# Where the key norms of the first four quads stand among vector, GpSimd and activation work

## The chip, the cores and the metric

The kernel runs on one core of one Trainium2 chip. The metric is the device time in microseconds (us), as the median of a few runs. The engines are named as in the profile: PE (TensorE, matmuls), PEld (its weight loads), DVE (VectorE), ACT (ScalarE), POOL (GpSimd) and SP (SyncE, which here only issues transfers). Each engine works through its own queue in order, and waits on semaphores for the others.

## The reference

Attention with normalised queries and keys (8 batches, 12 heads, 448 positions, head size 64) feeds a feed-forward block (3584 tokens, 768 to 1024 to 768) with a softmax-weighted activation and a layer norm.

```
def rmsnorm(x, g):
    rms = np.sqrt(np.mean(x * x, axis=-1, keepdims=True) + 1e-06)
    return x / rms * g
q_n, k_n = (rmsnorm(q, g_q), rmsnorm(k, g_k))
scores = scale * np.matmul(q_n, k_n.transpose(0, 1, 3, 2))
attn = softmax(scores);  out = np.matmul(attn, v)        # then per token:
h = x @ w_in;  e = np.exp(h - h_max);  solu = h * e / sum(e)
ln = (solu - mu) / np.sqrt(var + 1e-06) * g_ln;  return ln @ w_out
```

(The softmax is written out in the original, and the last two lines are shortened.)

## The kernel before

The attention part works on **quads**: 24 of them, each of two **pairs** of heads. Quad m has the pairs a = 2m and b = 2m + 1, so pair 3 is the second pair of quad 1, and quad 0 has the pairs 0 and 1. The loop over m writes its order out by hand: the order of the calls is the order of each engine's queue. What a pair goes through, with the lines of the profile:

- `load` (L634): eight transfers of 56 KB, issued by SP, bring the queries and keys into one of five buffers. `load_v` (L647, L651) brings the values of a quad.
- `squares` (L656): ACT squares all 128x896 numbers. `row_sums` (L664): DVE sums them by groups of 32. `fold_sums` (L674, L675): POOL adds the two halves of each row for both pairs of a quad; `fold_one` (L684, L685) does that for a single pair on DVE.
- `rsqrt_seed` (L694, L695): ACT takes a logarithm and an exponential. `rsqrt_step` (L701 to L704): four small DVE instructions refine the result. These two are the norms.
- `normalise` (L713): POOL multiplies the queries and keys by the norms. `qk_transpose` (L723): DVE transposes the product. `gain` (L727): ACT scales the queries.
- `scores` (L812) and `scores_last` (L825): PE makes a score tile; ACT takes its exponential (L802). A quad has seven of these: three for pair a, one shared by both pairs (the "last", or shared one), three for pair b.
- `add` (L839): DVE adds two exponentials of a pair. `outputs` and `values` (L854, L865): PE multiplies by the values. `sums` (L884): PE sums the exponentials with a matrix of ones. `inverse` (L895, L896, and four POOL copies L903) and `divide` (L910, L911) turn the sums into factors and apply them on DVE. `store_x` (L916) writes the quad's result to memory.

Score tiles and the tile of `sums` take turns in three PSUM buffers. So the third score tile of a quad (`scores(a, 2)`) is written to the buffer that held the sums of the quad before, and waits until DVE has read that at L895. Each score tile likewise waits for the exponential three tiles back.

`unit(...)` runs one piece of PE work and then whatever `later(...)` has set for that time; the `divide` of quad m comes in that way, after the first score tile of quad m + 1. `steps_at` lists the quads in which a piece of the input weights is converted (L535, L536 on ACT, L541, L542 on DVE); from quad 2 on it is one piece in each of quads 2 to 6. From quad 5 the squares of both pairs stand together (`scarce` is then false). `early` says that a quad makes the norms of the next at its very top.

After the attention come the feed-forward products (L982, and then L1177), with PE busy throughout.

Of the kernel before, what the change touches and what calls it, by code (L numbers as in the profile page):

```python
# [366 lines left out]
def fast_path(  # L367
# [252 lines left out]
    norms = {}  # L620
# [32 lines left out]
    def squares(n):  # L653
        d = st[n]
        d["sq"] = work.tile([P, 2 * NB, 32], FP32, tag="sq", name="sq", bufs=2)
        nc.scalar.activation(d["sq"], d["qk"].rearrange("p s b d -> p (s b) d"), AF.Square)  # L656
# [3 lines left out]
    def row_sums(n):  # L660
        m, i = divmod(n, 2)
        if i == 0:
            norms[m] = {"part": small.tile([P, 2, 2 * NB], FP32, tag="part", name="part", bufs=2)}
        nc.vector.tensor_reduce(norms[m]["part"][:, i], st[n]["sq"], AX, OP.add)  # L664
# [25 lines left out]
    def rsqrt_seed(d):  # L690
        ss = d["ss"]
        p, w = ss.shape
        y = d["y"] = small.tile([P, 4 * NB], FP32, tag="ny", name="ny", bufs=2)[0:p, 0:w]
        nc.scalar.activation(y, ss, AF.Ln, scale=1.0 / D, bias=eps[0:p])  # L694
        nc.scalar.activation(y, y, AF.Exp, scale=-0.5)  # L695
# [24 lines left out]
    def qk_transpose(n):  # L720
        d = st[n]
        d["qkT"] = work.tile([P, 2, S], FP32, tag="qkT", name="qkT", bufs=3)
        nc.vector.transpose(d["qkT"].rearrange("p s t -> p (s t)"), d["qkn"].rearrange("p b d -> p (b d)"))  # L723
# [80 lines left out]
    def scores(n, kc):  # L804
        d = st[n]
        s = ps_t.tile([P, 2, 512], FP32, tag="t", name="s")

        for c in range(0, P, D):
            for h in range(2):
                hh = slice(h * D, (h + 1) * D)  # L810
                keys = slice(NJ * c + kc, NJ * (c + D - 1) + kc + 1, NJ)
                nc.tensor.matmul(  # L812
                    s[c : c + D, h, 0:S], d["qkT"][hh, 1, keys], d["qkT"][hh, 0, :],
                    start=True, stop=True,
                )
        exponentials(d, kc, s)

    def scores_last(m):

        s = ps_t.tile([P, 2, 512], FP32, tag="t", name="s")  # L820
        for i in range(2):
            for h in range(2):
                hh = slice(h * D, (h + 1) * D)
                qkT = st[2 * m + i]["qkT"]
                nc.tensor.matmul(  # L825
                    s[i * D : (i + 1) * D, h, 0:S], qkT[hh, 1, NJ * P : S], qkT[hh, 0, :], start=True, stop=True
                )
        exponentials(quads[m], NJ, s)
# [7 lines left out]
    def add(n):  # L836
        d = st[n]
        d["es"] = work.tile([P, 2, S], FP32, tag="es", name="es")
        nc.vector.tensor_tensor(d["es"], d["E", 0], d["E", 1], OP.add)  # L839
# [433 lines left out]
    def unit(f, steps=4):  # L1273
        nonlocal now
        f()
        now += steps
        due = [x for x in todo if x[0] <= now]
        todo[:] = [x for x in todo if x[0] > now]
        for _, g in sorted(due, key=lambda x: x[0]):
            g()  # L1280
# [40 lines left out]
    with tc.manual_schedule():  # L1321
# [19 lines left out]
        for m in range(NQ):  # L1341
            a, b = 2 * m, 2 * m + 1

            def outputs():
                values_last(m)
                values(a)


            next1 = m + 1 < NQ
            next2 = m + 2 < NQ  # L1350
            next3 = m + 3 < NQ
            if m == 0:
                unit(lambda: scores(a, 0))
                normalise_rows(1, 0)
                normalise_rows(1, 1)
                unit(lambda: scores(a, 1))
                unit(lambda: scores(a, 2))
                for s in range(2):
                    transpose_rows(1, s)
                    take_rows(1, s)  # L1360
                squares(2)
                row_sums(2)
                fold_one(2)
                unit(lambda: scores_last(m))
                rsqrt_seed(norms["one", 2])
                rsqrt_step(norms["one", 2])
                normalise(2)
                add(a)
                unit(lambda: scores(b, 0))
                unit(lambda: scores(b, 1))  # L1370
                unit(lambda: scores(b, 2))
                squares(3)
                add(b)
                row_sums(3)
                qk_transpose(2)
                fold_one(3)
                gain(2)
                rsqrt_seed(norms["one", 3])
                rsqrt_step(norms["one", 3])
                normalise(3)  # L1380
                load_v(1)
                load(6)
                load(7)
                for _ in range(2):
                    load_next()
                unit(outputs)
                squares(4)
                row_sums(4)
                qk_transpose(3)
                gain(3)  # L1390
                unit(lambda: values(b))
                unit(lambda: sums(m))
                inverse(m)
                later(1, lambda m=m: divide(m))
                continue
            early = 2 < m and next1
            if early:
                rsqrt_seed(norms[m + 1])
                rsqrt_step(norms[m + 1])
                normalise(a + 2)  # L1400
                normalise(b + 2)
            for x in joins_at.get(m, ()):
                combine_in(x)
            if next1:
                load_v(m + 1)
            unit(lambda: scores(a, 0))
            store_x(m - 1)
            if early:
                qk_transpose(a + 2)
                if next3:  # L1410
                    load(a + 6)
            unit(lambda: scores(a, 1))
            if m == 1:
                squares(5)
                row_sums(5)
                fold_sums(2)
            unit(lambda: scores(a, 2))
            if m == 2:
                rsqrt_seed(norms[m + 1])
                rsqrt_step(norms[m + 1])  # L1420
                normalise(a + 2)
                normalise(b + 2)
            if m == 1:
                norm_gain()
            unit(lambda: scores_last(m))
            if m < 2:
                add(a)
            unit(lambda: scores(b, 0))
            if m == 1:
                rsqrt_seed(norms[m + 1])  # L1430
                rsqrt_step(norms[m + 1])
                normalise(a + 2)
                normalise(b + 2)
                load(a + 6)
                load(b + 6)
            if m == 2:
                qk_transpose(a + 2)
                load(a + 6)
            unit(lambda: scores(b, 1))
            if early or m == 2:  # L1440
                qk_transpose(b + 2)
                if next3:
                    load(b + 6)
            if m > 1:
                add(a)
            unit(lambda: scores(b, 2))
            if m == 1:
                qk_transpose(a + 2)
            scarce = m < 5
            if next2:  # L1450
                squares(a + 4)
                if not scarce:
                    squares(b + 4)
                row_sums(a + 4)
            if next1:
                gain(a + 2)
            if m == 1:
                add(b)
                qk_transpose(b + 2)
            if next1:  # L1460
                gain(b + 2)
            if scarce:
                squares(b + 4)
                if m > 1:
                    add(b)
            if next2 and m > 1:
                row_sums(b + 4)
                fold_sums(m + 2)
            if not scarce:
                add(b)  # L1470
            add_more(a)
            add_more(b)
            unit(outputs)
            step(m - 2)
            begin(m)
            step(m - 1)
            if m - 1 in sets:
                load_next()
            unit(lambda: values(b))
            if m == NQ - 1:  # L1480
                block_sums(0, 0)
                block_sums(0, 1)
                load_x(1)
            unit(lambda: sums(m))
            inverse(m)
            if m == 1:
                row_sums(b + 4)
                fold_sums(m + 2)
            if next1:
                later(1, lambda m=m: divide(m))  # L1490
            if m == NQ - 2:
                load_x(0)
                sizes(0)
# [191 lines left out]
```

## Time and profile before

| what | before |
|---|---|
| median of 3 runs | 822.98 us (822.57 to 824.52) |
| profiled execution, its own time | 821.82 us |
| its span in the profile | 819.3 us (2.52 us of the time lie around it) |
| PE busy | 800.6 us, 98% of the span |
| DVE busy | 672.4 us, 82% |
| POOL busy | 463.6 us, 57% |
| ACT busy | 461.0 us, 56% |
| mean share of the 16 DMA engines' time | q1 52.0%, q10 4.3% |
| TensorE clock granted | 0.995 |

A profile is of one execution. The median of the runs is 1.16 us above the time of the profiled one, so sums made in the profile are compared with its own time. Times inside it are in us from the start of the span. A timeline line has the start, the length, the engine, the line, the operation, what it writes and reads, and in square brackets the idle time before it and what ended that. A wait for several semaphores is put down to the one that came last by the profile.

The PE work of a quad is the same from quad to quad, and it begins with the first score tile. By the timeline of PE these begin at 10.19 (quad 0), 25.03, 43.74, 58.44, 72.72 and 85.62 us (quad 5); after that a quad takes 12.90 us each time, to the end of the attention.

### The profile page before, as it was taken

The numbers are of one execution on the slowest core, as the hardware profiler recorded it, in microseconds if no ns is written. First come the engines' busy times: TensorE is split into PE (matmuls) and PEld (weight loads), VectorE is DVE, ScalarE is ACT, GpSimd is POOL, SyncE is SP. The second block draws the span as 40 slices with busy tenths as digits, with TensorE's granted clock in tenths as the row PEclk, the third lists the DMA queues.
The fourth block names the chain that finished last, engine by engine and source line by source line (L and its number), as shares of the span: only waits on it lengthen the run. The fifth ranks groups of instructions, "written<-read, shape, count | busy, mean of one in ns | idle before, by whom it ended". The sixth has DMA issues, their size and how long they took to land.

```text
span 819.3 us, 14945 instructions
## 1 busy us (share of the span) xinstructions
PE 800.6 (98%) x5030; PEld 470.2 (57%) x5030; DVE 672.4 (82%) x1203; ACT 461.0 (56%) x757; POOL 463.6 (57%) x635
## 2 busy tenths in 40 slices
PE   8899999999999999999999999999899999999996
PEld 4333444444344443444444444444689999999996
DVE  6679897887878878589999999999996866866945
ACT  6568777786877766355655445442425454464420
POOL 1334556455554557222254378776487867777861
PEclk9999999999999999999999999999999999999999
DMA  6778777877778654225555434542448457366312
GB/s 132 144 166 184 155 195 157 184 156 153 174 154 184 143 136 123 82 82 168 153 149 145 132 90 125 152 135 72 140 149 276 136 195 252 116 234 211 118 59 82
DMA packets 271938, 122.74 MB, mean 150 GB/s; under 512 B 190444, under 2 KB 257004, under 8 KB 271852
## 3 DMA queue, kind: packets, MB, share of 16 engines
q1 hardware_dynamic: 256668, 111.79, 52.0%
q10 hardware_dynamic: 15184, 9.90, 4.3%
q8 instruction: 42, 0.69, 0.4%
q14 instruction: 44, 0.36, 0.1%
HBM read 84.94 MB, written 36.70 MB: 148 GB/s over the span
## 4 chain that ended last, share of the span: by engine, by line
PE 88%; DVE 3%; SPq 3%; POOL 2%; DMA 2%; issue 1%; ACT 0%; DVEq 0%; POOLq 0%
PE b L982 31%; PE A L1177 14%; PE o L865 12%; PE s L812 12%; PE B L1177 7%; PE sm L884 5%; PE C L1177 3%; SPq L634 3%; PE s L825 2%; PE o L854 2%; DMA v<-in_v_dram 1%; DMA qk<-in_k_dram 0%; POOL sums L1156 0%; POOL qkn L713 0%; POOL sums L1155 0%
## 5 line engine op out<-in xcount | busy, mean ns | idle before, releaser
L982 PE MATMUL b<-w_in,xg 128*128 128x512 f32 x336 | 151.1, 592 | 0.0
L802 ACT ACTIVATE E<-s 128x896 f32<-128x896 f32 x168 | 139.1, 935 | 14.2 <-PE s L812 13.7
L812 PE MATMUL s<-qkT 64*64 64x448 f32 x1152 | 121.2, 547 | 4.0 <-DVE r L895 2.8
L982 PE MATMUL b<-w_in,xsum 128*128 128x512 f32 x252 | 115.0, 592 | 0.0
L865 PE MATMUL o<-E,v 128*64 128x448 f32 x576 | 113.5, 543 | 0.0
L982 PEld LDWEIGHTS b<-w_in,xg 128*128 128x128 f32 x336 | 63.8, 190 | 80.2 <-issue 77.1
L674 POOL COPY ss<-part 32x56 f32<-32x56 f32 x88 | 42.6, 484 | 92.8 <-DVE part L664 90.0
L713 POOL TENSOR_TENSOR qkn<-qk,ny 128x896 f32<-128x896 f32 x46 | 78.0, 1715 | 23.0 <-DMA qk<-in_k_dram 17.3
L1177 PE MATMUL A<-w_out,sums 128*128 128x192 f32 x392 | 80.8, 329 | 4.0 <-ACT u L1189 2.6
L812 PEld LDWEIGHTS s<-qkT 64*64 64x64 f32 x1152 | 48.2, 163 | 63.4 <-ACT E L802 29.0
L982 PEld LDWEIGHTS b<-w_in,xsum 128*128 128x128 f32 x252 | 47.9, 190 | 60.3 <-issue 57.4
L1060 POOL TENSOR_TENSOR he<-he,mhalf 128x1 f32<-128x1 f32 x28 | 17.1, 610 | 114.5 <-DVE he L1059 112.5
L865 PEld LDWEIGHTS o<-E,v 128*64 128x64 f32 x576 | 39.2, 137 | 72.7 <-issue 65.7
L1177 PE MATMUL B<-w_out,sums 128*128 128x192 f32 x392 | 80.1, 327 | 0.0
L1066 ACT ACTIVATE u<-u,shift,he 128x1024 f32<-128x1024 f32 x28 | 34.7, 1239 | 74.9 <-POOL shift L1062 72.3
L1177 PEld LDWEIGHTS A<-w_out,sums 128*128 128x128 f32 x392 | 66.6, 191 | 5.3 <-issue 2.9
L1177 PEld LDWEIGHTS B<-w_out,sums 128*128 128x128 f32 x392 | 66.6, 191 | 0.2
L839 DVE TENSOR_TENSOR es<-E 128x896 f32<-128x896 f32 x48 | 53.9, 1125 | 0.5 <-ACT E L802 0.5
L664 DVE TENSOR_REDUCE part<-sq 128x28 f32<-128x896 f32 x46 | 48.5, 1080 | 5.5 <-ACT sq L656 3.5
L723 DVE STREAM_TRANSPOSE qkT<-qkn 128x896 f32<-128x896 f32 x46 | 48.6, 1089 | 4.5 <-POOL qkn L713 4.5
L563 POOL TENSOR_TENSOR w_out<-w_out 128x384 f32<-128x384 f32 x44 | 50.7, 1158 | 1.9
L1177 PE MATMUL A<-w_out,s 128*128 128x192 f32 x224 | 45.8, 327 | 0.6 <-ACT u L1189 0.6
(143 smaller groups left out, 1497.5 us busy)
## 6 DMA issues: line engine op xcount, KB each, us to landing
ur<-ud SPq DMA_DIRECT2D x60, 256.0 KB, 4.4
ud<-ub SPq DMA_DIRECT2D x112, 128.0 KB, 2.3
xd<-xo SPq DMA_DIRECT2D x24, 448.0 KB, 3.4
qk<-in_q_dram SPq DMA_DIRECT2D x184, 56.0 KB, 2.3
qk<-in_k_dram SPq DMA_DIRECT2D x184, 56.0 KB, 2.2
v<-in_v_dram SPq DMA_DIRECT2D x24, 384.0 KB, 4.4
out_dram<-P SPq DMA_DIRECT2D x21, 384.0 KB, 3.5
raw<-in_moe_w_in_dram SPq DMA_DIRECT2D x12, 512.0 KB, 4.6
```

The costliest lines, as they stand in the source:

```text
L563: nc.gpsimd.tensor_tensor(o, p, q, OP.subtract)
L664: nc.vector.tensor_reduce(norms[m]["part"][:, i], st[n]["sq"], AX, OP.add)
L674: e.tensor_copy(ss[g * 32 : g * 32 + 32], part[o * 32 : o * 32 + 32])
L713: e.tensor_tensor(d["qkn"], d["qk"].rearrange("p s b d -> p (s b) d"), y.rearrange("p b -> p b ()").to_broadcast([P, 2 * NB, 32]), OP.mult,)
L723: nc.vector.transpose(d["qkT"].rearrange("p s t -> p (s t)"), d["qkn"].rearrange("p b d -> p (b d)"))
L802: nc.scalar.activation(d["E", kc], s[:, :, 0:S], AF.Exp)
L812: nc.tensor.matmul(s[c : c + D, h, 0:S], d["qkT"][hh, 1, keys], d["qkT"][hh, 0, :], start=True, stop=True,)
L839: nc.vector.tensor_tensor(d["es"], d["E", 0], d["E", 1], OP.add)
L865: nc.tensor.matmul(d["o"][h * D : (h + 1) * D, :], quads[n // 2]["v"][:, n % 2 * 2 + h, kc], d["E", kc][:, h], start=False, stop=(kc == NJ ...
L884: nc.tensor.matmul(sm[g : g + 32, :], ones[:, w], e[:, h, t * S // 2 : (t + 1) * S // 2], start=(x == 0), stop=(x == len(terms) - 1),)
L982: nc.tensor.matmul(o, a[:, c], w_in[i][:, c], start=(c == 0), stop=(c == HD - 1))
L1177: nc.tensor.matmul(k[bank], a[:, c].rearrange("p a i -> p (a i)"), w_out[:, area, i, c], start=begin and c == 0, stop=c == KC - 1, skip_gr ...
```

## The change

It moves calls in quads 0 to 3. No instruction is added, removed or reshaped, and the order on PE and on SP's queue stays as it was; the order on DVE, ACT and POOL changes.

- Quad 0: `add(a)` goes ahead of the row sums of pair 2; the squares of pair 3 go behind the shared exponential, and its row sums and norms behind the next exponentials; the transposes of pair 2 and `add(b)` come after all norms. The squares of pair 5 move here from quad 1, behind the squares of pair 4, and the row sums of pairs 4 and 5 and their fold come after `inverse(m)`; the inverse then stands directly behind the transposes of pair 3 on DVE.
- Quad 1: what moved to quad 0 is gone.
- Quad 2: the norms (and the products of pairs 6 and 7) move from behind `scores(a, 2)` to behind `scores(a, 1)`.
- Quad 3: the norms move from the top of the quad to behind `scores(a, 0)`, which puts them behind `divide(2)` on DVE; the transposes of pair 8 and `load(a + 6)` move behind `scores(a, 2)`.

```
@@ quad 0
                 squares(2)
+                add(a)
                 row_sums(2)
                 fold_one(2)
                 unit(lambda: scores_last(m))
+                squares(3)
                 rsqrt_seed(norms["one", 2])
                 rsqrt_step(norms["one", 2])
                 normalise(2)
-                add(a)
                 unit(lambda: scores(b, 0))
+                row_sums(3)
+                fold_one(3)
                 unit(lambda: scores(b, 1))
                 unit(lambda: scores(b, 2))
-                squares(3)
-                add(b)
-                row_sums(3)
-                qk_transpose(2)
-                fold_one(3)
-                gain(2)
                 rsqrt_seed(norms["one", 3])
                 rsqrt_step(norms["one", 3])
                 normalise(3)
+                qk_transpose(2)
+                gain(2)
+                add(b)
                 load_v(1)
...
                 unit(outputs)
                 squares(4)
-                row_sums(4)
                 qk_transpose(3)
                 gain(3)
                 unit(lambda: values(b))
+                squares(5)
                 unit(lambda: sums(m))
                 inverse(m)
+                row_sums(4)
+                row_sums(5)
+                fold_sums(2)
                 later(1, lambda m=m: divide(m))
                 continue
@@ quads 1 to 3
-            early = 2 < m and next1
-            if early:
+            early = 3 < m and next1
+            def norms_next():
                 rsqrt_seed(norms[m + 1])
                 rsqrt_step(norms[m + 1])
                 normalise(a + 2)
                 normalise(b + 2)
+
+            if early:
+                norms_next()
...
+            if m == 3:
+                norms_next()
             unit(lambda: scores(a, 1))
-            if m == 1:
-                squares(5)
-                row_sums(5)
-                fold_sums(2)
+            if m == 2:
+                norms_next()
             unit(lambda: scores(a, 2))
-            if m == 2:
-                rsqrt_seed(norms[m + 1])
-                rsqrt_step(norms[m + 1])
-                normalise(a + 2)
-                normalise(b + 2)
+            if m == 3:
+                qk_transpose(a + 2)
+                load(a + 6)
...
-            if early or m == 2:
+            if early or 1 < m < 4:
                 qk_transpose(b + 2)
```

More of the change, by code (lines that the diff above doesn't have):

```diff
@@ L1429, in fast_path @@
             if m == 1:
[L1430 to L1433, printed above, removed]
+                norms_next()
                 load(a + 6)
```

## The prediction

> **What bounds the kernel now.** I first read the page's busy shares and its chain of waits.
>
> ```profile
> PE 800.6 (98%) x5030; PEld 470.2 (57%) x5030; DVE 672.4 (82%) x1203; ACT 461.0 (56%) x757; POOL 463.6 (57%) x635
> PE 88%; DVE 3%; SPq 3%; POOL 2%; DMA 2%; issue 1%; ACT 0%; DVEq 0%; POOLq 0%
> ```
>
> PE bounds the whole, so only time that PE lacks in the first quads can be gained. Next, the waits of PE from 12 to 70 us (waiting engine and line, releaser, us in total, times, longest):
>
> ```profile
> PE s L812 <- DVE r L895: 2.8, 1, 2.8
> PE s L825 <- ACT E L802: 1.5, 3, 1.0
> PE s L812 <- ACT E L802: 0.6, 1, 0.6
> PE sm L884 <- DVE es L839: 0.4, 1, 0.4
> ```
>
> From 63 to 560 us PE has no wait. Quads 1, 2 and 3 take 18.71, 14.70 and 14.28 us by their first score tiles (25.03, 43.74, 58.44, 72.72), an undisturbed one 12.90: together 9.0 us over. That is the ceiling. The timelines of PE and DVE show the largest piece:
>
> ```profile
> 29.59 1.59 PE L812 MATMUL s<-qkT 64*64 64x448 f32 x8 [2.79 <-DVE r L895]
> 26.71 1.09 DVE L664 TENSOR_REDUCE part<-sq 128x28 f32<-128x896 f32 x1 [0.39 <-ACT sq L656]
> 28.13 1.11 DVE L723 STREAM_TRANSPOSE qkT<-qkn 128x896 f32<-128x896 f32 x1 [0.33 <-POOL qkn L713]
> 29.17 0.37 DVE L895 STREAM_TRANSPOSE r<-sm 128x224 f32<-128x224 f32 x1
> ```
>
> The third score tile of quad 1 waits for L895, which stands on DVE behind the transpose of pair 3. The last question is what else is tight. SP issues without a break, so its transfers of pair 9 can't come earlier. Its issue, and ACT's square of that pair:
>
> ```profile
> 49.22 2.05 SPq L634 DMA_DIRECT2D qk<-in_k_dram  x4
> 55.51 0.94 ACT L656 ACTIVATE sq<-qk 128x896 f32<-128x896 f32 x1
> ```
>
> The last of these four is issued at 50.80 and lands 3.2 us later, at 54.0: the square has only 1.5 us in hand. And DVE and POOL in quad 3:
>
> ```profile
> 58.78 0.41 DVE L895 STREAM_TRANSPOSE r<-sm 128x224 f32<-128x224 f32 x1
> 60.44 0.19 DVE L701 TENSOR_SCALAR nx<-ss 128x56 f32<-128x56 f32 x1 [0.89 <-POOL ss L675]
> ...
> 64.28 2.16 DVE L723 STREAM_TRANSPOSE qkT<-qkn 128x896 f32<-128x896 f32 x2
> 66.37 1.05 DVE L839 TENSOR_TENSOR es<-E 128x896 f32<-128x896 f32 x1
> ```
>
> Between 60.44 and 64.28 DVE does the norms and then `divide(2)`, while POOL multiplies pair 8: the divide hides the product. DVE then runs without a pause but 0.17 us to its conversion at 70.58.
>
> **What the skill says.** The Trainium skill, "SBUF — State Buffer", section "SBUF: two separate sides", says that a VectorE instruction with two SBUF inputs and a GpSimd instruction take a shared port pair by exclusive lock. The trace agrees: the two adds from 18.47 take 3.59 us (two apart take 2.1), the product beside them 2.48 instead of 1.70. "TensorE: Matmul & The Clock Gate", section "What's actually happening", says that an idle window of about 3.4 us halves the PE clock. The trace agrees: after 26.48 to 29.90 us with 0.62 us of PE work, the clock is 0.50 for 3.41 us.
>
> **The change, part by part.** Nothing is added, so each part is an order, and I walk the queues with the durations of this trace. As steps between starts: exponential 0.80, square 0.84, ACT's gain 0.56, the two ACT steps of the norms 0.53, product 1.66 (1.70 long), transpose 1.04, add 0.99, row sums 1.00, POOL's fold 1.41 (2.20 beside a DVE instruction with two inputs), its inverse copies 0.89, divide 2.54, norms on DVE 1.1, conversion 1.42.
>
> 1. *Quad 0.* The add moved ahead starts at 14.28, with POOL idle. The square of pair 3 stands at 16.2, so its norms end on DVE at 21.7, its product runs from 21.8 to 23.5, and both transposes are done by 25.4. `add(b)` now stands at 22.7, inside that product: from 0 (it may wait nowhere) to 0.8 us (it waits until 23.5), taken 0.65. L895 follows at 25.4 instead of 29.17, so the third tile doesn't wait. The square of pair 5, now ahead of quad 1's first exponential, waits for its load until 26.4 (0.4 us); that exponential starts at 27.2 instead of 29.85. Then exponentials, 0.80 apart, limit PE: values of quad 1 at 32.1 instead of 35.6. The half clock costs up to 1.7 us of PE if it comes again.
> 2. *Quads 1 and 2.* Without the squares, sums and fold of pair 5 in quad 1 its norms start at 31.65 instead of 36.90. Quad 2 starts at 39.6, 4.1 us early. Its norms wait for POOL's fold until 43.2; the third exponential now stands behind them, and PE waits 1.35 us. Quad 3 starts at 53.8, 4.6 us early.
> 3. *The load.* ACT comes to the square of pair 9 at 50.9 and waits until 54.0: of 4.6 us, 1.4 are left. From here nothing ahead counts, up to 3 us of error in 1 and 2 included. Sums at 55.1, DVE's L895 at 56.1, fold on POOL 56.3 to 57.7. PE, ahead, waits 1.2 us for L895.
> 4. *The divide before the norms, in quad 3.* POOL's inverse copies stand behind the fold (57.7 to 58.6), so `divide(2)` runs from 58.6 to 61.15. Only then come the DVE norms: the product of pair 8 starts at 62.2, where before it started at 61.95. Nothing covers it on DVE now. Transposes at 63.9 and 65.6, adds and row sums from 66.6, conversion at 70.6: the start that it had before. The remaining 1.4 us is lost here. What it buys, the first exponential of quad 3 ahead of the norms, is worth little, as PE waits for the next ones (1.1 us).
> 5. *Quad 4 and after.* The fold (70.8, 2.20 long) and norms end at 73.5. PE starts quad 4 at 70.2 and waits 0.7 for L895 and 1.3 for the first exponential, which comes at 73.5, where before it came at 73.81 with PE's next tile 0.4 us slack. Quad 4's values start 0.4 us early, and from there both kernels are alike.
>
> Transfers moved: the eight of `load(a + 6)` in quad 3 move past score tiles in the program, but past nothing on SP's queue; POOL's queue keeps its order. Cover of the squares' move in quad 0 is the load of pair 9; without it the sum would be as in the first rival.
>
> Sum: minus 0.4 us on 821.82, the time of the profiled execution, gives 821.4. The median shown lies 1.16 above that execution, so I take 822.98 − 0.4 = **822.6 us**. A measurement of this kernel can tell about 0.3%, here 2.5 us, from no change.
>
> **The rivals.**
>
> *Held by the load, gain returned in quad 3* (the forecast). Each us by which the load of pair 9 lands elsewhere moves the end by one us. A landing of 2.2 us, usual in this queue, instead of 3.2 gives 821.6; with 1.1 us later 823.7. Own range 821.2 to 824.0. Chance 0.60.
>
> *The load lands early.* At 51.4 or before, the chain of step 3 begins at PE's own sums, and all else follows 2.6 us sooner: 3.0 us in all, 820.0. For it: nothing on SP waits for compute, and a landing depends on the traffic beside it. Against it: the issue alone ends at 51.3. Over 0.3% needs a landing before 51.9. In this case I also count errors of my walk in step 4, such as a fold ahead of its place. Chance 0.18.
>
> *The load lands late* (slower). In the kernel before, pair 9's load could be 1.5 us later at no cost; now it is on the path from the first. Place: quad 2's tail, ACT at L656. Price: the lateness less 0.4 us; slower by 0.3% from 2.9 us late, at 56.9. At 3.3 us late it gives 825.9. For it: the chain of waits has a transfer of the values stretched to 7.15 us, where the page has 4.4 as the median. The same holds for later loads, but with 0.4 us used of their slack. The half clock in quad 4, where PE idles some 3 us, would add to it: up to 1.7, by itself 824.3 and no verdict. Chance 0.15.
>
> ```profile
> 37.47 7.15 DMA v<-in_v_dram
> ```
>
> *The change doesn't part adds and products.* `add(b)` still meets the product in quad 0. Even if both double (1.1 and 1.7 us), that ends ahead of the 3 us wait of step 3: 822.6 again. Chance 0.07.
>
> **How the numbers follow.** Faster by over 0.3%: the early load, 0.18. Within: the forecast 0.60 and the last rival 0.07, so 0.67. Slower: 0.15. The range from 819.9 to 825.2 takes in the early load's value and stops short of the late one's; some 2 in 10 are left out.
>
> **What would show it.** In the changed profile: no wait of PE for L895 at quad 1; quad 2 starting near 39.6 and quad 3 near 53.8; ACT idle some 3 us before the square of pair 9, ended by a transfer; in quad 3 a DVE pause of 1.9 us before the transpose of pair 8; PE waits of about 1 us each at quads 3 and 4; quad 5 starting within 0.5 us of 85.6. If quad 5 starts at 83 and ACT doesn't wait for the transfer, the load is not the bound and I am wrong; if DVE reaches its conversion well before 70.6, step 4 is wrong.

## The result, and the profile after

The changed kernel took 822.78 us (median of 12 runs, 821.91 to 824.68), the kernel before 822.77 us (12 runs): a ratio of 1.000, 95% interval 0.999 to 1.001. Forecast was 822.6 us and no measurable change. The profiled execution took 822.29 us, with a span of 819.9.

The page of the changed kernel, busy shares and chain of waits:

```profile
PE 799.1 (97%) x5030; PEld 468.7 (57%) x5030; DVE 671.6 (82%) x1203; ACT 460.8 (56%) x757; POOL 462.0 (56%) x635
PE 87%; DVE 5%; POOL 2%; DMA 1%; issue 1%; SPq 1%; ACT 1%; DVEq 0%; POOLq 0%; ACTq 0%
```

PE still bounds the whole. Its waits from 12 to 70 us (total, times, longest):

```profile
PE sm L884 <- DVE es L839: 1.7, 2, 1.2
PE s L812 <- ACT E L802: 1.1, 2, 0.9
PE s L825 <- ACT E L802: 0.6, 1, 0.6
PE pg L476 <- ACT E L802: 0.3, 1, 0.3
```

The 2.8 us wait for L895 is gone, and the sum of what is listed fell from 5.3 to 3.7 us. But the list ends at 70 us, and waits of 1.00, 0.36 and 1.13 us follow in the changed kernel up to 75.42, where the kernel before has none. So nothing is won, as the first score tiles of the quads show (us in the profile):

| | quad 0 | 1 | 2 | 3 | 4 | 5 | quad 5 from quad 0 |
|---|---|---|---|---|---|---|---|
| before | 10.19 | 25.03 | 43.74 | 58.44 | 72.72 | 85.62 | 75.43 |
| after | 10.51 | 26.02 | 40.38 | 56.46 | 71.15 | 86.22 | 75.71 |

Quad 2 comes 3.4 us earlier. Of that, 2.0 are left at quad 3, 1.6 at quad 4, and none at quad 5; from there both kernels take 12.90 us a quad. The timeline of DVE shows three places of interest (the idle time before an instruction stands in brackets):

```profile
19.89 1.34 DVE L684 COPY ss<-part 32x28 f32<-32x28 f32 x4
...
23.67 1.78 DVE L839 TENSOR_TENSOR es<-E 128x896 f32<-128x896 f32 x1
...
26.40 0.37 DVE L895 STREAM_TRANSPOSE r<-sm 128x224 f32<-128x224 f32 x1
...
42.35 0.65 DVE L910 STREAM_TRANSPOSE r<-rc 128x448 f32<-128x448 f32 x1
45.45 0.63 DVE L911 TENSOR_TENSOR xo<-o,r 128x448 f32<-128x448 f32 x1 [2.46 <-DMA xd<-xo]
...
59.41 0.65 DVE L910 STREAM_TRANSPOSE r<-rc 128x448 f32<-128x448 f32 x1 [1.84 <-POOL rc L903]
...
61.97 0.18 DVE L701 TENSOR_SCALAR nx<-ss 128x56 f32<-128x56 f32 x1
...
64.84 1.11 DVE L723 STREAM_TRANSPOSE qkT<-qkn 128x896 f32<-128x896 f32 x1 [1.86 <-POOL qkn L713]
```

In quad 0, L895 stands at 26.40, as the change meant it. In quad 2, DVE stops 2.46 us in the middle of `divide(1)`, as L911 writes `xo`, of which there is one buffer, and the store of quad 0's result from it has not landed (issued at 38.62, landed at 45.36). In quad 3, DVE waits for POOL's inverse copies, divides, makes the norms, and waits 1.86 us for the product. ACT in quad 2:

```profile
50.09 0.95 ACT L656 ACTIVATE sq<-qk 128x896 f32<-128x896 f32 x1 [1.60 <-DMA qk<-in_k_dram]
...
53.59 0.95 ACT L656 ACTIVATE sq<-qk 128x896 f32<-128x896 f32 x1
```

The first is the square of pair 8, the second that of pair 9, which was forecast to wait 3 us for its load. It doesn't wait: the load landed at 53.49, just in time, because ACT itself came late. PE's own waits at the ends of quads 2 and 3 and in quad 4:

```profile
55.94 0.59 PE L884 MATMUL sm<-es,ones 128*32 128x224 f32 x8 [1.18 <-DVE es L839]
...
70.63 0.58 PE L884 MATMUL sm<-es,ones 128*32 128x224 f32 x8 [1.00 <-DVE es L839]
...
75.42 0.98 PE L825 MATMUL s<-qkT 64*64 64x448 f32 x8 [1.13 <-ACT E L802]
```

### The profile page after: what moved, and what is told of

Same layout as the page of the kernel before. It is cut to its first block, busy times and chain, and to the rows that moved or that the text cites. A ratio compares the mean times of both kernels' runs of the same rounds, so it can differ in the third digit from the quotient of the medians.

```text
span 819.9 us, 14946 instructions
## 1 busy us (share of the span) xinstructions
PE 799.1 (97%) x5030; PEld 468.7 (57%) x5030; DVE 671.6 (82%) x1203; ACT 460.8 (56%) x757; POOL 462.0 (56%) x635
## 4 chain that ended last, share of the span: by engine, by line
PE 87%; DVE 5%; POOL 2%; DMA 1%; issue 1%; SPq 1%; ACT 1%; DVEq 0%; POOLq 0%; ACTq 0%
PE b L982 31%; PE A L1177 14%; PE s L812 12%; PE o L865 11%; PE B L1177 7%; PE sm L884 5%; PE C L1177 3%; PE s L825 2%; PE o L854 2%; SPq L634 1%; DMA v<-in_v_dram 1%; DVE es L839 1%; PE pt L766 1%; DVE part L664 1%; DVE qkT L723 1%
```

## The experiments

Each kernel was timed against the kernel before on the same chip. *Lost later* is the time from quad 5 to quad 22 beyond the 219.25 us that both kernels need for it. The ratio with its interval is the measurement's own estimate, and is not the quotient of the two medians. Starts and *lost later* are of the profiled execution, which can be some us off the median: in e1 it took 826.53 us and in e7b 827.27, or 2.8 and 3.8 above the median, so what these two lost is more than usual; in e2 and e3 it lies within 0.4 of the median.

| run | quad 3 | quad 4 | quad 5 | lost later | median (before beside it) | ratio, 95% interval |
|---|---|---|---|---|---|---|
| e1_norms3_top | 57.26 | 71.54 | 84.43 | 5.64 | 823.75 (822.59) | 1.0004 [0.9988, 1.0019] |
| e2_xo_two | 54.35 | 69.07 | 84.14 | 3.21 | 824.11 (822.59) | 1.0009 [0.9995, 1.0022] |
| e3_raw_late | 54.82 | 69.49 | 84.56 | 3.94 | 824.72 (822.59) | 1.0018 [1.0005, 1.003] |
| e4_before_norms3_low | 58.66 | 73.33 | 88.41 | 0.30 | 824.76 (822.59) | 1.0016 [1.0005, 1.0026] |
| e5b_before_raw_act | 63.89 | 78.18 | 91.08 | 13.85 | 839.89 (822.58) | 1.0208 [1.0185, 1.0231] |
| e6b_raw_act | 62.52 | 76.74 | 91.81 | 9.20 | 838.48 (822.58) | 1.0198 [1.0182, 1.0214] |
| e7b_top_xo | 54.10 | 71.42 | 84.32 | 6.16 | 823.47 (822.58) | 0.9998 [0.9983, 1.0013] |
| e8b_top_xo_raw_act | 62.92 | 76.75 | 89.64 | 13.38 | 837.70 (822.58) | 1.0187 [1.0164, 1.021] |
| e9_top_xo_one_piece | 54.84 | 68.65 | 81.55 | 0.0 | 817.21 (822.48) | 0.9923 [0.9901, 0.9946] |
| e10_before_one_piece | 58.96 | 73.24 | 86.13 | 0.0 | 821.96 (822.48) | 0.9992 [0.9983, 1.0] |
| e11_one_piece | 54.34 | 69.02 | 84.10 | 0.0 | 820.55 (822.48) | 0.9967 [0.9955, 0.9979] |
| e12_top_xo_raw_pool | 55.20 | 68.89 | 81.79 | 1.49 | 819.48 (822.24) | 0.9966 [0.9952, 0.9979] |

### Where the first quads give the gain back

**Quad 3's norms back at the top** (e1), and, as its mirror, **only quad 3 of the change** put into the kernel before (e4):

```
-            early = 3 < m and next1        # e1; the other way round in e4
+            early = 2 < m and next1
-            if m == 3:
-                norms_next()
...
-            if m == 3:
-                qk_transpose(a + 2)
-                load(a + 6)
...
-            if early or 1 < m < 4:
+            if early or m == 2:
```

> The changed kernel with quad 3 alone put back as it was before the change (norms of quad 4 at the top of quad 3, so ahead of divide(2) on DVE). Theory A, the divide in quad 3 returns the gain: the fold of pairs 8 and 9 ends at 58.4 us as in the changed kernel, but the DVE norms follow at once, so the product of pair 8 starts near 60.0 instead of 63.11, the divide runs beside it, and the adds come some 3 us earlier. Quad 3 then lasts about 14.3 us as in the kernel before (instead of 14.69) and quad 4 about 13 (instead of 15.08): quad 5 starts near 83.8 instead of 86.22, and the median is near 820.4, 2.4 under the changed kernel. Rival B, the place of the norms in quad 3 is neutral, because the exponential that they delay costs PE what the norms gain: quad 5 stays within 0.5 us of 86.2 and the median near 822.8.

> The kernel before with the change's quad 3 alone (norms behind the first score tile, transposes and load moved with them). Theory A: quads 1 to 3 start as before (25.0, 43.7, 58.4); divide(2) starts behind GpSimd's inverse copies near 61.3 us, the DVE norms come near 63.9 instead of 60.44, the product of pair 8 near 65.0 instead of 61.95, the transpose near 66.7 instead of 64.28; quad 5 starts between 87.3 and 88.0 instead of 85.62, and the median is near 824.9, some 2.1 above the kernel before. Rival B, neutral: quad 5 within 0.5 us of 85.6, median near 822.8.

From quad 3's start to quad 5's the changed kernel takes 29.76 us and e1 27.17; the kernel before takes 27.18 and e4 29.75. So divide ahead of norms costs 2.6 us, in either surrounding. (Quad 2 of e4 came at 45.02, where 43.7 was expected: the clock was at 0.50 for 6.8 us in quad 1 instead of 3.4. By quad 3 only 0.2 us of this was left.) DVE's timeline in e4 gives the order that the forecast walked through, the divide behind POOL's copies, the norms 2.6 us behind that, the product bare:

```profile
61.60 0.65 DVE L910 STREAM_TRANSPOSE r<-rc 128x448 f32<-128x448 f32 x1 [1.82 <-POOL rc L903]
...
64.16 0.18 DVE L701 TENSOR_SCALAR nx<-ss 128x56 f32<-128x56 f32 x1
...
67.03 1.11 DVE L723 STREAM_TRANSPOSE qkT<-qkn 128x896 f32<-128x896 f32 x1 [1.86 <-POOL qkn L713]
```

Theory A holds for the quads. For the time it holds in e4 (slower, as expected), but not in e1: 820.4 us was expected, and 823.75 came, though quad 5 was 1.8 us earlier than in the changed kernel.

**Two buffers for `xo`** (e2), and **the second weight piece behind the load of pair 9** (e3):

```
-        xo = quads[m]["xo"] = work.tile([P, 2, S], FP32, tag="xo", name="xo", bufs=1)
+        xo = quads[m]["xo"] = work.tile([P, 2, S], FP32, tag="xo", name="xo", bufs=2)
```

```
-                for _ in range(2):
-                    load_next()
+                load_next()
...
                 load(a + 6)
                 load(b + 6)
+                load_next()        # quad 1
```

> The changed kernel with two buffers instead of one for the quad's result xo, so that divide(1) in quad 2 need not wait for the store of quad 0's result. Theory C, this store is what holds quad 2: L911 has no wait near 43 us (2.46 in the changed kernel), the product of pair 6 starts near 46 instead of 48.4, PE's wait of 1.2 us at the sums of quad 2 goes, quad 3 starts near 55.3 instead of 56.46; then the load of pair 9, landing near 53.5, is next, with L895 near 55.7; quad 5 starts near 85.1 and the median is near 821.7. Rival D, the forecast's load of pairs 8 and 9 alone is the bound: quad 3 stays at 56.2 to 56.5, quad 5 within 0.3 us of 86.2, the median near 822.8.

> The changed kernel with the second of the two 512 KB weight pieces (L510, issued at 36.35 us) issued behind the load of pair 9. It has 2.1 us of transfer at its own rate (two take 4.2). Theory E, transfers bound quad 2, by the store and by the loads together: the store of quad 0's result lands near 43.3 instead of 45.36, the loads of pairs 8 and 9 near 48 and 51.4 instead of 49.98 and 53.49; quad 3 starts near 55.3, its L895 stands near 54.9, and quad 5 near 84.6; median near 821.2. Rival, engines bound it (GpSimd's product and DVE): landings move but quad 3 and quad 5 don't, median near 822.8. If the piece is now late for its own conversion in quad 3 (ACT at 69 us), quad 4 would be later, which I don't expect: it lands near 57.

In e2 the wait for the store is gone on DVE, and what comes next is the load of pair 9, by way of ACT's square. First ACT, then DVE:

```profile
52.74 0.95 ACT L656 ACTIVATE sq<-qk 128x896 f32<-128x896 f32 x1 [0.78 <-DMA qk<-in_k_dram]
```

```profile
42.88 0.63 DVE L911 TENSOR_TENSOR xo<-o,r 128x448 f32<-128x448 f32 x1
...
53.73 1.09 DVE L664 TENSOR_REDUCE part<-sq 128x28 f32<-128x896 f32 x1 [0.42 <-ACT sq L656]
54.73 0.41 DVE L895 STREAM_TRANSPOSE r<-sm 128x224 f32<-128x224 f32 x1
```

Quad 3 starts at 54.35 instead of 56.46, quad 5 at 84.14. Theory C holds: the store was quad 2's bound. In e3 the same wait shrinks, with quad 5 at 84.56 where 84.6 was expected:

```profile
43.82 0.62 DVE L911 TENSOR_TENSOR xo<-o,r 128x448 f32<-128x448 f32 x1 [1.22 <-DMA xd<-xo]
```

But neither median is below the kernel before, and they are 2.4 and 3.5 us above what was expected.

### Where the rest goes

So 1.7 to 2.1 us were won by quad 5 in e1, e2 and e3 against the changed kernel, and lost behind it. ACT's waits from 87 to 325 us in e1 (total, times, longest), and the same kind from 90 to 290 us in the kernel before:

```profile
ACT sq L656 <- DMA qk<-in_k_dram: 11.7, 11, 2.4
```

```profile
ACT sq L656 <- DMA qk<-in_k_dram: 0.4, 1, 0.4
```

The chain of waits from 100 to 290 us says it too. In the kernel before it is PE alone:

```profile
by line: PE o L865 36.8%; PE s L812 36.4%; PE sm L884 15.0%; PE s L825 5.9%; PE o L854 5.9%
```

In e1 it runs through SP's queue of loads:

```profile
by line: SPq L634 27.8%; PE o L865 12.5%; PE s L812 10.6%; DMA v<-in_v_dram 9.9%; DMA qk<-in_k_dram 5.6%; PE sm L884 5.4%; issue 5.3%; POOL ss L674 5.0%; PE s L825 2.7%; ACT sq L656 2.5%; PE o L854 2.4%; DVE part L664 2.3%; ACT E L802 1.9%;
```

From this came theory F: SP's queue keeps its own pace, with almost no lead over PE in the kernel before. There the square of pair 23 begins 0.02 us behind the landing of its load, and those of pairs 31 and 39 0.3 us behind theirs:

```profile
145.34 0.95 ACT L656 ACTIVATE sq<-qk 128x896 f32<-128x896 f32 x1 [0.43 <-DMA qk<-in_k_dram]
```

By this theory, whatever PE wins early it loses again at a load. To show it, SP has to be relieved. The first try had **ACT issue the weight pieces** (in the kernel before as e5b, in the changed kernel as e6b, and in e1 with two `xo` buffers as e8b; e7b is that last kernel without the relief):

```
         if src is moe_w_in:
-            nc.sync.dma_start(to, w[c * P : (c + 1) * P])
+            nc.scalar.dma_start(to, w[c * P : (c + 1) * P])
```

> The kernel before, with all twelve weight pieces (L510) issued by ACT instead of SP. A control. Theory F, SP's queue of transfers paces the attention and a lead over it is lost again: here PE has no lead, so quad 5 stays near 85.6 us, a quad 12.90, quad 23 near 317.1, and the median within 1 us of the kernel before; SP's loads of the second pairs land earlier (the square of pair 43 with several us in hand instead of some tenths to 1 us). Rival G, a piece on ACT's queue delays ACT or takes the bandwidth elsewhere: slower by 1 us or more.

> The changed kernel, with all weight pieces issued by ACT. Theory F: the first two are off SP's queue, so the store of quad 0's result lands before 43 us, quad 3 starts near 54.5 to 55.3, quad 5 near 84.3 (86.22 in the changed kernel), and this lead stays to quad 23 (near 315.8), as no square of a second pair waits for its load; median near 820.9. Rival G, losses in the later quads have another cause than SP's queue (ACT's own order, or the bandwidth shared by all queues): the lead is lost again before quad 23, with periods above 12.90, median 822 to 825.

> The changed kernel with quad 3's norms at the top as before the change and two buffers for xo; the weight pieces stay with SP. By the first quads: quad 3 near 54.4, quad 4 near 68.7, quad 5 near 81.6, four us ahead of the kernel before. Theory F: squares of second pairs (11 or so of them) wait for their loads between quads 6 and 21, quads last more than 12.90, and quad 23 starts at 317 to 321, so the lead is lost or more; median 821.5 to 824.5. Rival H, a lead once won is kept: quad 23 near 313.1, median near 818.6.

> The kernel of the run with quad 3's norms at the top and two xo buffers, and all weight pieces issued by ACT. Theory F: quad 5 near 81.5 and quad 23 near 313, since SP's queue has some 2 us more in each quad that loads a piece; median near 818.8, about 4 under the kernel before. Rival G: SP is no longer late but the quads still last more than 12.90 for another cause, quad 23 at 316 or later, median 821.5 or more.

All three with ACT's queue were 2% slower, the control too, so they decide nothing between F and G. SP's waits in the control, e5b, from 12 to 325 us, show where time goes:

```profile
SPq L469 <- DMA raw<-in_moe_w_in_dram: 9.8, 1, 9.8
SPq L634 <- DMA raw<-in_moe_w_in_dram: 7.8, 4, 2.7
```

By the profile SP waited for pieces that it had not issued. The longest of these waits, 9.8 us, begins in quad 0, with the loads queued behind it; quad 1 takes 25.35 us.

e7b tells two things. It lost 6.16 us behind quad 5, as F said. And with the store's wait and quad 3's divide out of the way, quad 2 ends where the forecast had seen it end, at the load of pair 9, landing at 53.99. ACT:

```profile
54.09 0.95 ACT L656 ACTIVATE sq<-qk 128x896 f32<-128x896 f32 x1 [2.26 <-DMA qk<-in_k_dram]
```

and DVE:

```profile
55.08 1.09 DVE L664 TENSOR_REDUCE part<-sq 128x28 f32<-128x896 f32 x1 [2.02 <-ACT sq L656]
56.08 0.41 DVE L895 STREAM_TRANSPOSE r<-sm 128x224 f32<-128x224 f32 x1
```

Quad 4 then starts at 71.42, not at the expected 68.7. In quad 3 PE waits 0.67 us for L895 and 1.65 for an exponential, and the clock is 0.50 from 59.1 to 62.5 us. By an estimate (half of these 3.4 us) that costs up to 1.7 us more, as the prediction had it for a half clock.

The second try **loads only the first piece**, so that no other queue takes the rest: in e7b's kernel (e9), the kernel before (e10) and the changed kernel (e11). It leaves out eleven of the twelve pieces, so the weights are not the reference's, and these three serve as measurements only.

```
-            raws.append(load_w(wq[len(raws)]))
+            raws.append(raws[0] if 0 < len(raws) < n_in else load_w(wq[len(raws)]))
```

> The kernel with quad 3's norms at the top and two xo buffers, and of the twelve weight pieces of the attention only the first is loaded; the other conversions read that piece again, so the weights are not the reference's, and the engines' work is the same. SP's queue has eleven 512 KB transfers less, with no other queue burdened. Theory F, SP's queue paces the attention and takes back any lead: the load of pair 9 lands near 52 instead of 53.99, quad 4 starts near 68.7 and quad 5 near 81.6, all later quads last 12.90, quad 23 starts near 313.1, and the median is near 818.3, over 4 under the kernel before. Rival G, the later quads' waits have another cause (ACT's or DVE's own order once PE is ahead): periods above 12.90 remain, quad 23 at 316 or later, median 821.5 or more.

> The control: the kernel before with only the first weight piece loaded (the other conversions read it again, so the weights are not the reference's). If fewer transfers alone made a kernel faster, this one would be too. Theory F says that the kernel before has no lead for SP to take back: quad 5 near 85.6, quad 23 near 317.1, median within 0.7 us of the kernel before, the square of pair 43 with several us in hand. Rival: the transfers slow the engines beside them everywhere, so it gains 2 us or more, and the run with the two other edits gains by that, not by its lead.

> The changed kernel as it is with only the first weight piece loaded (the other conversions read it again, so the weights are not the reference's). It loses the second 512 KB in front of the store of quad 0's result. Theory F with the store as the bound of quad 2: the store lands near 43.2 instead of 45.36, quad 3 starts near 54.8, quad 5 near 84.5, all later quads last 12.90, quad 23 near 316.0, median near 820.9. Rival G: quad 5 near 84.5, but quad 23 at 317.5 or later, and the median 822 or more.

This decides for F and against G. In e9 quad 5 starts at 81.55 and quad 23 at 313.06 (81.6 and 313.1 were expected), in e11 at 84.10 and 315.61 (84.5 and 316.0). Every quad behind lasts 12.90 us, and the lead stays to the end: 5.3 and 1.9 us faster than the kernel before beside them. The control gains only 0.5 us, with an interval that reaches 1.0, so fewer transfers don't make the kernel faster by themselves. The spread shrinks too: six executions of e9 took 816.47 to 817.49 us, those of e7b 820.02 to 827.27. What e9 to e11 can't tell is whether the pieces hurt by their place in SP's queue or by their traffic, as both are gone. SP's waits from 90 to 290 us in e9 show a queue that is now ahead, held by the divide (L911) 15 times; the kernel before has no such wait there:

```profile
SPq L916 <- DVE xo L911: 18.3, 15, 2.0
```

**A version with all its work done.** e7b with the pieces issued by GpSimd, so that the traffic stays and only SP's queue is relieved:

```
-            nc.sync.dma_start(to, w[c * P : (c + 1) * P])
+            nc.gpsimd.dma_start(to, w[c * P : (c + 1) * P])
```

> The kernel with quad 3's norms at the top and two xo buffers, with all work done and all twelve weight pieces loaded, issued by GpSimd instead of SP. In the run with the pieces on ACT's queue SP waited for the pieces' landings all the same. If GpSimd's queue is apart from SP's, theory F gives nearly the times of the run with one piece: quad 5 near 82, quad 23 near 313.5, median near 818.5, faster than both kernels. If SP waits for these pieces too, or if GpSimd's issuing delays its folds and inverse copies (they stand right behind), quads last more than 12.90 and it is slower than the kernel before by 5 us or more.

819.48 us, 0.9966 [0.9952, 0.9979] of the kernel before, and so faster than the changed kernel too, whose ratio is 1.000. Against the kernel before beside them, the medians of e7b, e12 and e9 are 0.9 us above, 2.8 below and 5.3 below: the place in SP's queue looks like the larger part, and the rest may be the traffic or GpSimd's issuing. The kernel before with its pieces on GpSimd was not run; with eleven of them left out (e10) it gained 0.5 us. Quad 5 starts at 81.79. 1.49 us are lost later, all by quad 9: from 81 to 140 us squares still wait, 4.0 us in all, mostly for transfers of the values and loads. What the piece costs GpSimd (its timeline in quad 0; the page's list of transfers with the median us to landing):

```profile
24.55 1.33 POOL L510 DMA_DIRECT2D raw<-in_moe_w_in_dram  x2
```

```profile
raw<-in_moe_w_in_dram POOLq DMA_DIRECT2D x12, 512.0 KB, 4.7
```

## Why the prediction was right, point by point

The time was right, and so was its form: time won in quads 0 and 1 is given back by quad 5. Of the two mechanisms behind that, the divide ahead of the norms in quad 3 was right, and the load that was to hold quad 2 was not the one at work: a store was. That the time came out is in part luck. Without the store's wait quad 5 starts at 84.14 (e2), 1.5 us ahead of the kernel before, and not within 0.5 us of 85.6. And the median would have said the same either way: e1, e2 and e7b reach quad 5 with a lead of 1.2 to 1.5 us, and their medians are no lower than that of the kernel before.

- *What bounds, and the ceiling.* Right: L895 is off the path in quad 1, and PE still bounds the rest. But "from 63 to 560 us PE has no wait" was read as safety. It hid a second limit with almost no margin, SP's queue.
- *Step 1.* The order came true. L895 came at 26.40 instead of 25.4. Of that, 0.32 is the later start of quad 0; 0.62 are the four copies of `fold_one(3)`, which now run beside a product and take 1.34 us instead of 0.72. The walk had priced contention for the add only (1.78 us measured, within its bounds). The half clock of quad 1 didn't come again. It is in every profile with the old order of quad 0 and in none with the new one, but for e6b and e8b, where ACT issues the pieces. The mean granted clock is the last number but two of these lines (30 to 34 us, the kernel before, then the changed one):

```profile
30.00:34.00 4.00, 3.78 (x25) 0.94 (x21) 2.93 (x5) 3.78 (x6) 0.76 (x4) 0.59 0.66 108
30.00:34.00 4.00, 4.00 (x42) 1.51 (x36) 3.37 (x8) 3.70 (x8) 0.69 (x3) 1.00 0.68 110
```

- *Step 2.* This one failed. Quad 2 was due at 39.6 and came at 40.38, close enough; quad 3 was due at 53.8 and came at 56.46. The step let `divide(1)` run without a wait. In the kernel before, L911 in quad 2 runs at 47.44 with the store landed at 46.11, 1.3 us of margin that the walk never looked at; 3.4 us earlier there is none. Without that wait quad 3 starts at 54.35 (e2).

```profile
47.44 0.62 DVE L911 TENSOR_TENSOR xo<-o,r 128x448 f32<-128x448 f32 x1
```

- *Step 3.* Right as a limit, not as the limit. The load landed at 53.49, half a us earlier than forecast, and was hidden by the later store. Where the store is out of the way (e7b), row sums and L895 stand at 55.08 and 56.08, forecast 55.1 and 56.1. So close a match is of one execution: in e2, whose order is the same up to there, the load landed at 52.64 and L895 stood at 54.73. So the two limits lie 0.7 to 2.1 us apart in L895 (56.80 in the changed kernel), and the store that the walk missed stood in for a load that can land 1.4 us earlier than forecast.
- *Step 4.* Right. DVE's pause ahead of the transpose is 1.86 us (forecast 1.9), norms at 61.97 and product at 63.11, 0.8 to 0.9 behind the forecast, as L895 was already (0.7). e1 and e4 put the loss at 2.6 us.
- *Step 5.* Right in kind: PE waits 0.36 for L895 and 1.13 for the exponential in quad 4. Quad 5 came 0.6 us later than before, or 0.28 counted from quad 0's start, where 0.4 earlier was forecast. At 86.22 it lies just outside the 0.5 us around 85.6 that the prediction had named as a sign.
- *The rivals.* "The load lands early" was priced as if a lead at quad 5 reached the end. e1, e2, e3 and e7b had 1.1 to 1.5 us of it against the kernel before, and lost 3.2 to 6.2 later in their profiled executions. Some executions seem to have kept theirs: the fastest of these four took 820.02 to 820.85 us, while the fastest of the kernel before beside them took 821.45 and 822.02. A lead of 3 us with SP's queue as it is was not run. "The load lands late" had the right thought in its last lines, that later loads have some tenths of slack as well, but used it only for the slower side. The adds and products did still meet, as the last rival had it, and that didn't decide.

The loss later can exceed the lead: in e1 SP's last load of pair 31 is issued at 197.47, in the kernel before at 192.88. Why SP itself falls behind there was not settled; the runs of these four kernels spread from 820 to 827 us, so the loss may well differ from one execution to the next.

## What to carry to other kernels

An engine that is busy for 98% of the time can have a second queue beside it that runs at the same pace, as SP's did here. Before you price an early gain, read the margin of that queue at each point where the two meet (landing against first use, over all stages, not only near the change), and every single-buffer write against the store that frees it. If the margin is some tenths of a us, relieve the queue first: here the same edits gave nothing with SP carrying the weight pieces and 0.34% with GpSimd carrying them. And an instruction moved ahead of its neighbour takes away the cover that the neighbour had from it: `divide(2)` hid a product, and ahead of the norms it hid nothing.

## What the runs showed of the hardware

- Copies with one input were slowed by a product on GpSimd: four copies of 32x28 took 1.34 us beside it and 0.72 apart. The product ends at 20.64 us, the copies at 21.23. The Trainium skill, "SBUF — State Buffer", section "SBUF: two separate sides", gives the lock to VectorE instructions in a 2-port performance mode too, and names 32-bit copies within SBUF as such; the trace agrees. The row sums beside the same product took 1.08 us, as they do alone.
- The same section warns that a transfer issued by GpSimd can stall, because GpSimd can't write descriptors while VectorE holds the ports. No such stall shows in e12's median: the pieces landed in 4.7 us, from SP in 4.8 (the changed kernel), and each took GpSimd 0.60 us. The slowest took 6.7 us to land, one of the two that quad 0 issues. Whether VectorE held the ports while GpSimd issued is not shown.
- With the pieces on ACT's queue, SP waited for their landings (9.8 us in one wait, e5b); with the pieces on GpSimd's, it did not (e12). No run shows why SP waits for what ACT has issued.
